# A block-sparse attention with two feed-forward layers: all steps in another searched order

## The chip, the cores and the metric

The kernel runs on one core of a Trainium2 chip. The metric is the time of the whole program on the device in microseconds (us), the median of three runs. The names of the engines are those of the profile: PE is TensorE (matmuls), PEld its weight loads, DVE is VectorE, ACT is ScalarE, POOL is GpSimd, and SP is SyncE, whose queue issues every DMA of this kernel.

## The reference, cut to what matters

```
# q, k, v: 2 batches x 8 heads x 768 positions x 64
k_sum = max of k over blocks of 32; v_sum = mean of v over the same blocks
scores = concat(local scores, banded to |i-j| < 16;  q @ k_sum + log(32)) / sqrt(64)
a = softmax(scores);  attn = a @ concat(v, v_sum)
x = attn as 1536 tokens x 512
h = x @ w_in (512 x 2048);   g = relu(h)**2;            x = g @ w_out (2048 x 512)
h = x @ w_in2;   g = h if h >= 1 else 0 if h <= -1 else (h+1)**2/4;   out = g @ w_out2
```

## The kernel before, in words

The attention is cut into 24 units, one for each pair of heads and each 256 queries. A unit has a score product (`S`, line 602), a max with mask (`M`, 610), an exponential (`E`, 616), a division (`R`, `N`), a transposition (`T`, 632), a value product (`O`, 643) and a split of the result into a high and a low part (`oh`, `ol`). These products are plain float32. Before the first value product the sums of `v` over the blocks must stand in the value tile (`v`, `vj`, and `f` on line 675).

The feed-forward products run as three products of high and low parts. Layer 1 begins with 24 units of 256 tokens (`H` on line 280 upwards, `Y` on line 407 downwards), which are mixed with the attention units. All other upward products (`Pa` to `Pg`, line 312) are one-level Strassen products of six matmuls, 384 tokens wide. Their sums and copies in PSUM are done by ACT and DVE (`Ca`, `Cc`, `Vb`, `Vc`, then `ha`, `hb`, `hc`, `hh`, `hl` for the activation and the split). A `Y` unit of layer 1 has 12 matmuls of 384 columns (256 in the mixed part). A `Y` unit of layer 2 has 9 matmuls of 512 columns.

The weights arrive as float64. For each of 64 tiles there is a load (`wl`, line 201), two steps on ACT (`dl`, `dq`), three on DVE (`dr`, `ds`, `dt`: lines 214, 216, 218), one on POOL (`da`, line 221) and a split (`wh`, line 235, and `wo`, line 240), with more sums for the Strassen products (`sa`, `sh`, `sl`).

The results of layer 2 are added up in SBUF (`ya`, line 432) and stored by rows of 128 tokens (`yd`, line 446). The last 128-token rows of the last group are made by four `Z` units (line 464: `Z0` and `Z1` are 12 matmuls of 512 columns, `Z2` and `Z3` the two halves of the third row block with 12 of 256), added by `za` (line 468) and stored by `zd` (line 473).

What sets the order is a table written out by hand, `PLAN`. It has one word for each step, and the program issues the steps in that order, each on its own engine. An engine works off its instructions strictly in that order, and so does SP's queue: a store that waits for its addition holds every DMA behind it. The last letter of a word (a, v or g) chooses ACT, DVE or POOL where a step can run on more than one.

Of the kernel before, what the change touches and what calls it, by code (L numbers as in the profile page):

```python
# [61 lines left out]
warm11 kl0 cl0 qf0 kl1 wl0 kl3 cl1 qf1 kl2 ql1 nl0 wl1 vl0 vl1 vl2 wl2 kl5 wl3 km0 S0 M0 km1 S1 E0 M1 dl0 km3 S3 dq0  # L62
E1 dr0 R0 M3 N0g km2 S2 E3 R1 ds0 N1g S5 M2 dq1 T1 R3 E2 N3v dt0 T3 T0 M5 da0 S7 to3a to0v E5 R2 S4 M7 N2g v0 dr1 T2
E7 wh0v v1 M4 wo0g R5 E4 R7 ds1 to1v v2 dt1 S6 N5v vc0 R4 dq2 wh1v vj0 N4g M6 vk0 dl1 vf0 vf1 ql2 wl4 dr2 E6 wl5 f0v
da1 kl6 to2v O0 ds2 O2 oh0v dt2 T4 oh2a O3 R6 to4a ol0 N6g oh3v dq3 O4 ol2 dl2 T5 ol3 dr3 S8 oh4a wl6 da2 ql3 vf2 f1a
ol4 to5a M8 O1 wh2a wo1g O5 oh1a T6 oh5a ol1 H1 dq4 ds3 wo2g to6v E8 ol5 S10 dr4 dt3 O6 N7v dl3 ds4 T7 dl4 M10 wl7 da3
bl0 kl4 vl3 wh3a S9 to7a dt4 H0 oh6a dq5 R8 ol6 E10 N8g M9 O7 S11 wo3g ha0v T8 ha1v oh7v hb1 wh4v da4 hb0 km5 dl5 hh0a
ol7 H2 hh1a dr5 hl0g to8a M11 E9 H3 hl1g ds5 wo4g km4 O8 S12 R10 ha2a ha3a R9 Y0 hb2 dt5 N9g oh8a hh2a km6 dq6 H4 E11
M12 hl2g da5 T9 vs0 S13 Y1 ha4a wh5a to9a bl1 dq7 wl8 Y2 wo5v wl9 ql4 kl7 vp0 vl4 hb3 dr6 E12 dr7 R11 H5 N10v N11g M13
# [732 lines left out]
```

## Time and profile before

| | us |
|---|---|
| median of 3 runs (lowest, highest) | 595.39 (595.04, 596.54) |
| the profiled execution | 594.42 |
| its span, first to last instruction | 592.6 |
| PE busy in the span | 569.6 |
| DVE, ACT, POOL busy | 474.7, 373.9, 243.5 |
| last matmul ends | 582.2 |

The profiled execution took 1.8 us more than its span and 0.97 us less than the median. "Busy" counts an engine's own instructions. Waits and DMA issues are not in it.

### The profile page before, as it was taken

What the parts mean: (1) busy time and instruction counts of PE and PEld (TensorE: products, weight loads), DVE (VectorE), ACT (ScalarE), POOL (GpSimd) and SP (SyncE); (2) the same over time, 40 slices, a digit from 0 to 9 for tenths busy, and PEclk for the clock granted to TensorE, in tenths of its full rate; (3) what the DMA queues carried; (4) which work ended last, traced back from release to release, by engine and by line L of the source; (5) the groups of instructions that cost most, each with busy time, mean ns of one, the idle gap of its engine ahead of it and who ended that gap; (6) DMA issues with size and microseconds to landing.
All of it is one profiled execution on the core that took longest, in us unless ns stands there. A gap on an engine that the chain in (4) does not pass through costs nothing.

```text
span 592.6 us, 11185 instructions
## 1 busy us (share of the span) xinstructions
PE 569.6 (96%) x4202; PEld 527.9 (89%) x4202; DVE 474.7 (80%) x1097; ACT 373.9 (63%) x866; POOL 243.5 (41%) x207
## 2 busy tenths in 40 slices
PE   6889999999999999999999999999999999999992
PEld 3578999999999999999999999888898998989982
DVE  5989889889989899768788999779897979666541
ACT  5778778757766455334657688877776656664430
POOL 0456464746563443415555566433431425121000
PEclk7899999999999999999999999999999999999997
DMA  8795711222122222112110302222211112000005
GB/s 321 283 297 133 228 46 40 90 72 73 71 72 72 107 107 72 71 51 94 72 72 1 117 26 72 71 72 71 89 54 72 72 36 105 3 1 2 1 1 212
DMA packets 16418, 52.17 MB, mean 88 GB/s; under 512 B 2124, under 2 KB 2732, under 8 KB 16364
## 3 DMA queue, kind: packets, MB, share of 16 engines
q1 hardware_dynamic: 16364, 51.45, 25.1%
q8 instruction: 33, 0.54, 0.4%
q14 instruction: 21, 0.17, 0.1%
HBM read 47.37 MB, written 3.15 MB: 85 GB/s over the span
## 4 chain that ended last, share of the span: by engine, by line
PE 84%; DVE 6%; DMA 5%; ACT 2%; issue 1%; SPq 0%; ACTq 0%; DVEq 0%
PE bank L407 40%; PE bank L312 31%; PE bank L280 5%; PE bank L602 3%; DMA raw<-in_wd_dram 2%; PE bank L632 2%; PE bank L643 2%; DMA k<-in_kd_dram 2%; PE bank L464 1%; DMA q<-in_qd_dram 1%; DVE fx L214 1%; DVE ks L590 1%; DVE fx L218 1%; DVE s L610 1%; ACT fr L207 1%
## 5 line engine op out<-in xcount | busy, mean ns | idle before, releaser
L221 POOL TENSOR_TENSOR fr<-fx,fr 128x512 uint32<-128x512 uint32 x64 | 84.6, 1333 | 152.6 <-DVE fx L218 82.9
L375 DVE TENSOR_TENSOR gl<-bank,gh 128x384 fp32r<-128x384 f32 (+1 forms) x124 | 65.8, 538 | 14.2 <-ACT gh L371 12.9
L312 PE MATMUL bank<-xh,wih 128*128 128x384 f32 x224 | 75.8, 339 | 0.5 <-DVE bank L325 0.5
L312 PE MATMUL bank<-xl,wih 128*128 128x384 f32 x224 | 75.2, 336 | 0.0
L350 ACT ACTIVATE tm<-bank,bias 128x384 f32<-128x384 f32 x62 | 35.9, 579 | 50.7 <-PE bank L312 41.2
L407 PE MATMUL bank<-gh,woh 128*128 128x384 f32 (+1 forms) x288 | 66.2, 321 | 0.0
L407 PE MATMUL bank<-gl,woh 128*128 128x384 f32 (+1 forms) x288 | 65.1, 317 | 0.0
L407 PE MATMUL bank<-gh,wol 128*128 128x384 f32 (+1 forms) x288 | 65.1, 317 | 0.0
L212 ACT ACTIVATE fx<-raw 128x512 f32<-128x512 f32 x64 | 42.5, 670 | 25.3 <-DMA raw<-in_wd_dram 19.5
L312 PE MATMUL bank<-xh,wil 128*128 128x384 f32 x224 | 57.1, 335 | 0.0
L312 PE MATMUL bank<-th,wih 128*128 128x384 f32 x168 | 56.3, 335 | 0.2 <-DVE bank L319 0.2
L312 PE MATMUL bank<-tl,wih 128*128 128x384 f32 x168 | 56.4, 336 | 0.0
L407 PE MATMUL bank<-woh,gh 128*128 128x512 f32 x180 | 56.0, 392 | 0.0
L407 PE MATMUL bank<-wol,gh 128*128 128x512 f32 x180 | 56.0, 392 | 0.0
L407 PE MATMUL bank<-woh,gl 128*128 128x512 f32 x180 | 56.0, 392 | 0.0
L432 DVE TENSOR_TENSOR acc<-bank,acc 128x384 f32<-128x384 f32 (+1 forms) x81 | 47.1, 603 | 8.7 <-PE bank L407 8.6
L367 DVE SCALAR_TENSOR_TENSOR bank<-bank,tm 128x384 f32<-128x384 f32 x64 | 35.5, 561 | 23.1 <-ACT tm L363 23.0
L407 PEld LDWEIGHTS bank<-gh,woh 128*128 128x128 f32 x288 | 48.9, 188 | 0.6
L407 PEld LDWEIGHTS bank<-gh,wol 128*128 128x128 f32 x288 | 49.0, 189 | 0.0
L407 PEld LDWEIGHTS bank<-gl,woh 128*128 128x128 f32 x288 | 49.0, 189 | 0.0
L207 ACT ACTIVATE fr<-raw 128x512 uint32<-128x512 uint32 x64 | 42.3, 668 | 5.8 <-DVE fx L216 2.1
L218 DVE SCALAR_TENSOR_TENSOR fx<-raw,fx 128x512 uint32<-128x512 uint32 x64 | 44.7, 706 | 0.4
(147 smaller groups left out, 1431.2 us busy)
## 6 DMA issues: line engine op xcount, KB each, us to landing
raw<-in_wd_dram SPq DMA_DIRECT2D x64, 512.0 KB, 4.6
k<-in_kd_dram SPq DMA_DIRECT2D x8, 400.0 KB, 6.5
out_dram<-acc SPq DMA_DIRECT2D x11, 256.0 KB, 2.8
q<-in_qd_dram SPq DMA_DIRECT2D x5, 512.0 KB
vw<-in_vw_dram SPq DMA_DIRECT2D x3, 768.0 KB, 7.0
vw<-in_vw_dram SPq DMA_DIRECT2D x2, 1024.0 KB
acc<-in_vb_dram SPq DMA_DIRECT2D x2, 768.0 KB
acc<-in_vw_dram SPq DMA_DIRECT2D x1, 1024.0 KB
```

The source lines that it names most:

```text
L207: A.activation(fr[n % 2], w_raw(n, 0), AF.Copy, scale=2.0 ** -29)
L212: A.activation(f32(x), f32(hi), AF.Abs)
L218: V.scalar_tensor_tensor(x, hi, 0xC0000000, x, ALU.bitwise_and, ALU.bitwise_or)
L221: G.tensor_tensor(fr[n % 2], fx[n % 2], fr[n % 2], ALU.add)
L280: PE.matmul(h_bank(n), a, b, start=i == 0, stop=i == len(ops) - 1)
L312: PE.matmul(q_bank(q, role), a, b, start=bool(first and i == 0), stop=i == 5, skip_group_check=not first)
L350: A.activation(a, h, AF.Relu, bias=bias[:, 1:2], scale=-1.0)
L367: V.scalar_tensor_tensor(h, h, 1.0, a, ALU.max, ALU.mult)
L375: e.tensor_tensor(lo, h if m else a, f32(hi), ALU.subtract)
L407: PE.matmul(ys[j], a, b, start=f == 0 and i == 0 and (n >= 24 or j % 2 == 0), stop=f == GF - 1 and i == 2 and (n >= 24 or j % 2 == 1))
L432: V.tensor_tensor(a, y_bank(g, t, j), a, ALU.add)
L602: PE.matmul(sbank(i, 2 * h + t)[r * 64:r * 64 + 64, 0 if keys else KW:KW if keys else KN], qs[cc % 2][rows, p, j * QT:(j + 1) * QT], b, st ...
```

## The change

Only the table `PLAN` changes. It holds the same 2277 steps, each once, with the same counts on the chip. They stand in another order, and of the steps that can run on several engines some run on another one. In the tail of the table the stores moved behind the additions that they need:

```
-hc133 ha135a hh133v Y129 hb135 hc135 hh135a Y130 hl135 hc134 hh134a Y131 ya104 hl134 ya106 hl133 Z0 Z3 Z1 za3 ya105 Z2
-za1 za0 zd1 yd105 yd101 yd96 zd3 yd104 yd100 yd98 yd102 yd106 yd97 za2 zd2 zd0
+ha135a hc134 hl131 Y129 hh134v hb135 hc135 hh133v Y130 hh135v hl135 hl134 ya102 Y131 ya104 hl133 yd104 yd101 yd100
+ya105 Z0 ya106 yd106 yd96 yd98 Z1 za0 zd0 yd102 yd97 yd105 Z2 za1 zd1 Z3 za2 zd2 za3 zd3
...
```

The end of SP's queue, before. L201 is the last load of weights, L473 a store of the last row blocks (`zd`), L446 a store of another row block (`yd`):

```order
L201 DMA raw_75<-in_wd_dram 128x1024 [waits DMAHW3_49]
L473 DMA out_dram<-acc 128x512 [waits DVE_49,Pool_49]
L446 DMA out_dram<-acc 128x512 x3
L473 DMA out_dram<-acc 128x256
L446 DMA out_dram<-acc 128x512
L446 DMA out_dram<-acc 128x512 [waits DMAHW5_49]
L446 DMA out_dram<-acc 128x512 [waits DMAHW6_49]
L446 DMA out_dram<-acc 128x512 [waits DMAHW7_49]
L446 DMA out_dram<-acc 128x512 [waits DMAHW0_49]
L446 DMA out_dram<-acc 128x512 [waits DMAHW1_49]
L473 DMA out_dram<-acc 128x256 [waits DMAHW2_49,DVE_49]
L473 DMA out_dram<-acc 128x512 [waits DMAHW3_49]
```

The same place now, without that load:

```order
L446 DMA out_dram<-acc 128x512 [waits DVE_49,Pool_49]
L446 DMA out_dram<-acc 128x512 [waits Pool_49]
L446 DMA out_dram<-acc 128x512
L446 DMA out_dram<-acc 128x512 [waits DVE_49]
L446 DMA out_dram<-acc 128x512 x2
L473 DMA out_dram<-acc 128x512 [waits DMAHW5_49,DVE_49]
L446 DMA out_dram<-acc 128x512 [waits DMAHW6_49]
L446 DMA out_dram<-acc 128x512 [waits DMAHW7_49]
L446 DMA out_dram<-acc 128x512 [waits DMAHW0_49]
L473 DMA out_dram<-acc 128x512 [waits DMAHW1_49,DVE_49]
L473 DMA out_dram<-acc 128x256 [waits DMAHW2_49,DVE_49]
L473 DMA out_dram<-acc 128x256 [waits DMAHW3_49,DVE_49]
```

Before, the first of the 13 stores is `zd1`, and it waits for `za1` on DVE. Now the first is `yd104`, which waits for `ya104`, and the four `zd` stand in the order in which their `Z` units end.

The first step on weights among DVE's work, before, as its 24th instruction. L590 is a maximum of a tile of `k`, L610 the mask and maximum of a score unit, L621 and L622 the division, L214 a step on the first tile of weights:

```order
L610 ISA sm_138 128x1
L590 TENSOR_REDUCE ks_123<-k_115 128x24
L214 TENSOR_SCALAR fx_76<-fx_76 128x512
L621 TENSOR_SCALAR sm_137<-sm_137 128x4
L622 RECIPROCAL sm_137<-sm_137 128x4
L610 ISA s_131,sm_140<-bank_65,cst 128x120
```

Now it is the fifth (L216, L218 and L235 are the next steps on the same tile):

```order
L214 TENSOR_SCALAR fx_76<-fx_76 128x512
L590 TENSOR_REDUCE ks_120<-k_112 128x24
L216 TENSOR_SCALAR fx_76<-fx_76 128x512
L218 SCALAR_TENSOR_TENSOR fx_76<-raw_74,fx_76 128x512
L590 TENSOR_REDUCE ks_123<-k_115 128x24
L235 CAST wih_80<-fx_76 128x512
L590 TENSOR_REDUCE ks_121<-k_113 128x24
L610 ISA s_128,sm_137<-bank_68,cst 128x120
```

The work on the first tile of weights, whose load is now the first DMA, moved ahead of the first score units' maxima.

A piece of the difference on PE in layer 2, between two `Y` units (L407), where two Strassen products (L312) are taken out and put elsewhere:

```order
 L407 MATMUL bank_63<-wol_86,gh_90 128x512
-L312 MATMUL bank_67<-th_1919,wih_81 128x384
-L312 MATMUL bank_67<-tl_1920,wih_81 128x384
-L312 MATMUL bank_67<-th_1919,wih_81 128x384
-L312 MATMUL bank_67<-tl_1920,wih_81 128x384
-L312 MATMUL bank_67<-th_1919,wil_83 128x384 x2
-L312 MATMUL bank_68<-xh,wih_1605 128x384
-L312 MATMUL bank_68<-xl,wih_1605 128x384
-L312 MATMUL bank_68<-xh,wih_1605 128x384
-L312 MATMUL bank_68<-xl,wih_1605 128x384
-L312 MATMUL bank_68<-xh,wil_1606 128x384 x2
 L407 MATMUL bank_65<-woh_84,gh_88 128x512
```

The two `Y` units around it now follow each other. Counted over the table, a `P` run is followed by a `Y` run 34 times in layer 2, and 44 times before. Between float32 attention products and the high-low products PE changes 35 times, and 47 times before.

## Rows read from the trace of the kernel before

**Rows 1.** The page: busy time, share of the span, instructions, by engine

```profile
PE 569.6 (96%) x4202; PEld 527.9 (89%) x4202; DVE 474.7 (80%) x1097; ACT 373.9 (63%) x866; POOL 243.5 (41%) x207
```

**Rows 2.** Windows: length, busy of PE, PEld, DVE, ACT, POOL, granted clock, DMA share, GB/s

```profile
0.00:15.00 15.00, 9.30 (x135) 5.46 (x139) 7.79 (x38) 7.73 (x28) 1.43 (x6) 0.78 0.88 323
15.00:30.00 15.00, 12.13 (x218) 7.80 (x210) 13.96 (x66) 10.75 (x46) 6.75 (x6) 0.84 0.76 280
30.00:45.00 15.00, 13.09 (x260) 11.23 (x260) 13.19 (x47) 11.69 (x34) 8.56 (x7) 0.93 0.92 296
45.00:60.00 15.00, 13.68 (x185) 12.82 (x179) 13.95 (x48) 12.43 (x45) 8.78 (x9) 1.00 0.54 133
60.00:575.00 515.00, 514.28 (x3388) 484.40 (x3387) 423.10 (x895) 331.31 (x716) 217.95 (x181) 1.00 0.19 65
```

**Rows 3.** PE's waits over the span: waited for, us, times, longest

```profile
PE bank L643 <- DVE vw L675: 2.9, 1, 2.9
```

**Rows 4.** DVE from 15 to 60 us, by form: busy us, mean ns, idle before

```profile
L218 DVE SCALAR_TENSOR_TENSOR fx<-raw,fx 128x512 uint32<-128x512 uint32 x7 | 4.7, 678 | 0.0
L216 DVE TENSOR_SCALAR fx<-fx 128x512 uint32<-128x512 uint32 x6 | 4.7, 784 | 0.0
...
L681 DVE TENSOR_REDUCE acc<-acc 96x64 f32<-96x2048 f32 x1 | 2.3, 2275 | 0.0
...
L635 DVE COPY pt<-bank 120x512 f32<-120x512 f32 x3 | 2.1, 688 | 0.4 <-PE bank L632 0.4
```

**Rows 5.** DVE from 60 to 580 us, by form

```profile
L240 DVE TENSOR_TENSOR wol<-fr,woh 128x512 fp32r<-128x512 f32 x13 | 9.7, 752 | 0.6 <-PE bank L407 0.6
```

**Rows 6.** Waits of SP's queue over the span

```profile
SPq L473 <- DVE acc L468: 80.9, 1, 80.9
...
SPq L797 <- DMA out_dram<-acc: 2.1, 1, 2.1
```

**Rows 7.** SP's timeline at the end: start, length, what (each is a DMA's issue)

```profile
581.53 0.35 SPq L473 DMA_DIRECT2D out_dram<-acc  x1
...
587.86 1.28 SPq L473 DMA_DIRECT2D out_dram<-acc  x2
```

**Rows 8.** DVE's timeline at the end

```profile
572.50 0.69 DVE L432 TENSOR_TENSOR acc<-bank,acc 128x512 f32<-128x512 f32 x1 [1.52 <-PE bank L407]
...
578.02 0.42 DVE L468 TENSOR_TENSOR acc<-bank,acc 128x256 f32<-128x256 f32 x1 [3.00 <-PE bank L464]
...
580.76 1.85 DVE L468 TENSOR_TENSOR acc<-bank,acc 128x512 f32<-128x512 f32 x3 [1.73 <-PE bank L464]
```

**Rows 9.** PE's timeline at the end, first matmul of Z0 and of Z3

```profile
573.66 0.39 PE L464 MATMUL bank<-woh,gh 128*128 128x512 f32 x1
...
576.38 0.28 PE L464 MATMUL bank<-woh,gh 128*128 128x256 f32 x1
```

**Rows 10.** The stores: us from issue to landing

```profile
DMA to landing us min/median/max: 2.4/2.8/3.1
```

**Rows 11.** The chain that ended last: start, us, what; from 60 us

```profile
79.75 1.62 PE bank L280 x12
...
119.20 1.44 PE bank L280 x12
...
312.12 2.38 PE bank L312 x12
...
347.94 2.08 PE bank L407 x9
350.02 1.06 PE bank L312 x6
...
460.10 4.18 PE bank L312 x24
...
563.58 10.24 PE bank L407 x45
573.83 8.34 PE bank L464 x48
```

More of the change, by code (lines that the diff above doesn't have):

```diff
@@ L157 @@
[L157 to L160 removed]
+warm11 wl0 kl0 qf0 kl3 kl1 cl0 qf1 wl1 ql1 kl2 wl2 vl0 nl0 vl1 vl2 wl3 dl0 dq0 dr0 km0 ds0 dt0 km3 da0 S0 wh0v wo0g
@@ new lines @@
+km1 S1 M0 dl1 M1 S3 E1 M3 E0 R1 km2 S2 N1g E3 R0 S5 M2 ql2 kl4 cl1 N0g T1 M5 dq1 S7 dq2 dr1 R3 E2 ds1 N3v T0 dt1 T3
+dr2 v0 E5 da1 to3v M7 v1 R2 ds2 dl2 S4 wh1v to1a wo1v E7 to0v R5 dt2 v2 N2v wh2a da2 M4 T2 vc0 dq3 R7 vj0 S6 to2v vk0
+N7g E4 M6 vf0 vf1 kl5 wl4 ql3 wl6 kl6 wl5 kl7 vf2 N5g f1v f0v O1 E6 R4 O3 N4v O2 dr3 T4 ds3 O0 to4a oh2v R6 oh0a ol2
+T5 N6g oh1a ol0 S8 oh3a ol1 to5a ol3 O4 dq4 M8 wo2g T6 oh4a S9 to6a ol4 dr4 E8 S10 dt3 T7 M9 O5 H1 ds4 oh5a to7a ol5
+R8 dl3 dt4 O6 dl4 da3 M10 H0 E9 bl0 wl7 oh6v N8g ol6 km5 S11 ha0a da4 O7 wh3a ha1v T8 hb1 oh7v hh1a R9 ol7 H2 wh4a
@@ new lines @@
+to13a R15 ug0v dl8 dq9 dr8 Y7 ub0v yo7a N14v S16 ds8 ol12 yo5a S17 O13 M16 ha9a T14 hb9 H10 oh13a hh9v hb8 M17 hl9g
+hh8a hl8v N15g E17 Y8 to14v ol13 uh0v H11 E16 R17 dt8 S18 uc0v S19 ha11a R16 ui0a dr9 O14 N16g M18 T15 oh14a Y9 ha10a
+to15v uj0g E18 ol14 M19 O15 ds9 T16 N17g hb11 oh15v S20 hb10 ol15 to16a R18 S21 E19 da8 T17 M21 O16 N18g H12 M20 E21
+uk0v H15 dt9 oh16a to17v wl11 hh10a wl10 da9 vl5 S23 E20 ol16 R19 S22 ul0v O17 N19g T18 LW0 wh8a M22 H14 hh11a to18a
+wh9v um0a R20 wo9g oh17v H13 hl11v ha12a saa2g ol17 dq10 R21 hl10g E22 O18 ha14v wo8v sab2g T19 Y10 un0v N20g hb12
@@ new lines @@
+hl18 ug1g wo10v Y17 hb19 wh13a da13 ha21v dl12 hh19v Y18 hl19 ds12 dt12 H22 ue0v wh12a wl14 da12 hb21 hh21a Y19 ha20v
+wo13v uh1g wo12v H23 saa3g ui1a Pc0 hb20 uj1v ha22a sab3v hb22 Pb0 yo19a Cc0v uk1v Pd0 dq15 Vb0 ul1g ha23a dr15 hh20a
+Pf0 hh22a sac3v sh7a hl20 Y20 dq14 hl21 sl7g hl22 ha24a dr14 um1a hb23 Y21 un1g ha25v ds14 hb25 sad3g hh23a Pa1 hb24
+hl23 hh25a uo1g hh24v Pe0 hl24 hl25 up1g Y22 Vc0 uq1v ha26a dt14 hb26 Y23 ds15 Ca1a sh6v hh26a dt15 sl6g hl26 Pd1
+yo23v ur1g Pc1 dl14 wh15v wh14a wl16 Pb1 ua2g Cc1a ha28v dl15 Pg0 hb28 ub2g Vb1 wl17 Pf1 da14 ha27v hh28v Pe1 uc2v
@@ new lines @@
+Pb5 dr25 dq24 wo23v Cc5a dr24 Y39 dl25 ds25 Vb5 hh43a ds24 ya14 Pd5 ya13 ya12 Pf5 dt25 ha44v da25 Pe5 hl43 ha45a ya15
+hb44 hb45 dt24 Y40 hh44a wl26 wh25a wl27 da24 hl44 hh45a wh24v wo25g Pa6 wo24v Y41 saa6v hl45 sab6g Vc5 Ca6a sac6v
+ha46a Pg5 sad6g hb46 dq27 hh46v Pb6 ha47a hl46 sh12v sh13v Pc6 sl13v Pd6 Cc6a hb47 Vb6 Y42 hh47v ha48a dr27 hb48 sl12v
+hh48a hl47 dl27 ds27 Y43 dt27 ya16 wh27a wl29 da27 dq26 Pf6 ya19 wo27g ya18 Pa7 hl48 ha49v dr26 Pe6 hb49 ya17 dl26
+ds26 Y44 dt26 Vc6 wl28 da26 hh49v ha50a wh26a Pg6 dq29 wo26v hb50 dr29 Y45 hl49 Ca7v dq28 ha51a dr28 Pd7 hh50a ds29
@@ new lines @@
+hb51 ds28 dt29 hh51a Y46 dl29 wh29v dt28 wl31 da29 ha52v hl50 hb52 Pb7 hh52a wo29g dl28 hl52 Pc7 hl51 wl30 da28 Y47
+Cc7a dq31 ya20 Vb7 wh28v saa7v Pe7 wo28g ya23 dq30 Pf7 Vc7 sab7g ya21 Pg7 dr31 sac7g Pa8 sad7v ha55a dr30 ha53a ya22
+hb55 Y48 sh15a hb53 sl15v sh14a ha54v sl14v Y49 hb54 hh53a hh55v dl30 ds31 hh54a hl54 Y50 hl55 hl53 Ca8a Pb8 Y51 ya25
+ds30 Pc8 dt30 ya26 wl32 Pd8 ya24 ya27 Cc8v Y52 ha56a dt31 dl31 Vb8 hb56 wl33 da31 wh30a hh56v Y53 hl56 da30 wh31a Pf8
+dq32 dr32 wo30v Pe8 ha57a dq33 Y54 hb57 dr33 wo31v hh57a Vc8 hl57 ha58a Pg8 ds32 hb58 dt32 dl33 Pa9 hh58v ds33 hl58
@@ new lines @@
+Y55 dt33 ha59v wh33a da33 Ca9a ya29 dl32 Pc9 hb59 wo33v wl34 da32 wl35 ya28 Pb9 wh32v Cc9a Pd9 Vb9 wo32v Pf9 ha60a
+ya30 saa8v hb60 ya31 Pe9 hh60a sab8g ha61v hl60 sac8g Y56 dq35 hh59v dq34 sad8g Vc9 sh17a hl59 hb61 dr35 sl17g sh16a
+Y57 ds35 dl35 dr34 dt35 hh61a Pg9 ha62a da35 Pa10 ha63v hl61 hb63 Y58 hb62 Ca10v wh35a hh62v hh63a hl62 ds34 sl16v
+Pc10 dt34 Pd10 Cc10a dl34 Pb10 wh34a ha64v wl36 da34 wl37 hl63 hb64 Y59 Vb10 wo35g ya32 yb32a hh64a wo34g ya34 Pf10
+ya33 ya35 yc32g Y60 hl64 yb34v ha65v dq37 dq36 Pe10 yb35a dr36 dl37 dr37 yb33v dl36 Y61 ds37 yc33g Vc10 hb65 ds36
@@ new lines @@
+ds39 Y68 dt39 hh72a hb73 hl72 wl41 da39 yb41a Vc12 wh38v Y69 hc73 dq40 ha74a dr40 wo38v Y70 wh39v hb74 yc41v yb42a
+hc74 yb40a ds40 hh74a wo39v dl40 Y71 yc40v dq41 dt40 dl41 dr41 wl42 da40 hh73a ya45 yb43a Pa13 ya44 wh40a ds41 uf4g
+ya46 Pg12 ya47 yb46a hl74 Y72 ha75a dt41 hl73 ui4a wl43 da41 Ca13v wh41a Pc13 ua4v dq42 wo41g hb75 Pb13 Cc13a hc75
+yb47a yc42g hh75a Pd13 Vb13 dq43 wo40v yc43g Pf13 ha76a hl75 Pe13 uj4g hb76 ha77a hc76 Pa14 hh76v saa10g hb77 Y73 hl76
+hc77 yc46g Vc13 hh77a yc47v ha78a sab10v Pg13 uk4v hb78 Y74 sac10v um4a hl77 dr43 Ca14a un4g hc78 ha79a hh78v Pd14
@@ new lines @@
+Pf17 sab12v ya60 sac12g Pg17 ha93a dr50 sad12g ds50 Y88 hb93 sh25v ha94a dt50 hc93 Y89 sl25v hh93a hb94 hl93 ha95a
+dr51 hc94 sh24v Y90 dl51 hh94v hb95 ds51 Ca18a hl94 dt51 Pd18 hc95 wh51a wl53 da51 hh95v Pc18 ha96a hl95 sl24g Pb18
+Cc18v hb96 wh50a hc96 Y91 wo51v dq53 ya64 dl50 Vb18 hh96a wl52 da50 dl53 Pa19 hl96 wo50g Pe18 Pf18 Vc18 ya65 ha98a
+Pg18 dr53 ds53 dq52 Y92 ha97a dr52 dt53 wl55 hb97 dl52 Y93 hc97 hh97a ha99a hl97 ds52 Y94 dt52 Ca19a hb98 ya66 wl54
+da52 hb99 hc98 wh52v hh98a Pd19 wh53a hl98 wo52g hc99 Pb19 ha100a da53 Pc19 hh99a hb100 Y95 hc100 Cc19a wo53v hh100a
@@ new lines @@
+Vb19 saa13g hl99 hl100 sab13g Pf19 ya68 sac13g sh27v Pe19 ha101a sad13v sl27g ya70 Pa20 ya69 Y96 Vc19 ha102a hb101 Y97
+hb102 hc101 hc102 hh101a hh102a hl101 hl102 Ca20a Pg19 sh26v sl26g Pc20 ha103a Pd20 Cc20a hb103 Pb20 dq55 hc103 dl54
+dr55 Y98 dq54 hh103a dr54 ha104a Vb20 ds54 hl103 Y99 dl55 ds55 ya72 dt55 Pf20 ya73 da55 dt54 Pa21 ha105a ya74 Pe20
+wl56 wl57 da54 hb104 hb105 hc104 Y100 hc105 hh104a hh105v hl104 wh54a Vc20 Y101 hl105 dq56 ha106a wh55v wo54v dq57
+Y102 wo55v hb106 Ca21a dr57 dl57 ds57 hc106 Pd21 dt57 hh106a dr56 wl59 Pg20 da57 hl106 ha108a wh57v Pb21 hb108 ds56
@@ new lines @@
+wo57g ha107a hc108 Pc21 dt56 saa14g hh108v Y103 Cc21a hl108 dq59 Vb21 dl56 wh56v hb107 ya76 wl58 da56 Pf21 ya77 hc107
+Pe21 wo56g hh107a ha109a Y104 Vc21 sab14v hl107 hb109 dq58 hc109 ha110a dr59 Pa22 ds59 dr58 Pg21 dt59 hb110 hc110 Y105
+hh109v ha111a hl109 Ca22v hh110a sac14v hb111 sh29v Y106 sad14v sl29g hc111 sh28a ds58 hh111a wh59a Pd22 hl110 dt58
+Pc22 sl28v ha112a Pb22 Cc22v dl59 hl111 hb112 wl61 da59 Y107 dl58 hc112 Vb22 hh112a wl60 da58 ya80 wh58a hl112 Pe22
+Pf22 dq61 Vc22 ya81 ha114a Pg22 ya78 ha113a Pa23 hb114 Y108 hb113 hc114 hc113 hh114a dq60 hl114 hh113a Y109 ha115a
@@ new lines @@
+hl113 dr60 dr61 Ca23a ya82 hb115 Pb23 ds61 wo59v ds60 Pd23 dl61 dt60 dt61 Pc23 ha116a hc115 wl63 da61 Y110 hb116 hc116
+wo58g hh116v Cc23v Y111 dl60 Vb23 hh115a hl116 wl62 da60 wh61v Pf23 hl115 wo61v Pe23 saa15v ha117a sab15g Pa24 Vc23
+wh60a ya85 dq63 Pg23 ya84 dq62 wo60v ha118a Y112 sh31a hb117 sl31g hb118 hc117 Y113 ha119a sac15g sad15g hh117a Y114
+hl117 hc118 Ca24a hb119 hh118v hc119 Pd24 hl118 ya86 Pc24 ha120a Pb24 hh119a Cc24a hl119 Y115 hb120 Vb24 sh30a dr62
+ya88 hc120 Pf24 sl30v hh120v Pe24 hl120 ha121a ya89 Pa25 Vc24 hb121 hc121 Pg24 hh121a ha122a Y116 ha123v hb122 Y117
@@ new lines @@
+hc122 hb123 hh122v dr63 hl121 Y118 Ca25v hl122 ya90 hc123 Pb25 ds62 hh123v Pc25 ds63 dt62 hl123 Pd25 Cc25v Vb25 Y119
+ha124a ya92 hb124 hc124 Pf25 ya93 hh124a hl124 Pe25 ha125a dt63 Pa26 Vc25 wh62a ya94 hb125 Pg25 ha126a hc125 hh125v
+Y120 dl63 hl125 hb126 da63 Ca26v hc126 hh126a Pd26 ha127a hl126 Pb26 hb127 dl62 Pc26 hc127 ha128a da62 Y121 Cc26v
+wh63a Vb26 wo62g hb128 hh127a hl127 Pf26 wo63g hc128 Pe26 ha129a Pa27 hb129 hh128a hc129 Y122 hl128 hh129a hl129 Y123
+ya96 ya97 Y124 Ca27v ya98 Vc26 ha130a Y125 hb130 hc130 Pd27 hh130a hl130 Pg26 ha132a Pb27 ha131v Pc27 Y126 Cc27v hb131
@@ L161 @@
+hb132 hc132 Vb27 Y127 hh132v hl132 ya100 hc131 Pe27 ya101 hh131a Pf27 Vc27 ha134v Pg27 ha133a Y128 hb133 hc133 hb134
+ha135a hc134 hl131 Y129 hh134v hb135 hc135 hh133v Y130 hh135v hl135 hl134 ya102 Y131 ya104 hl133 yd104 yd101 yd100
+ya105 Z0 ya106 yd106 yd96 yd98 Z1 za0 zd0 yd102 yd97 yd105 Z2 za1 zd1 Z3 za2 zd2 za3 zd3
 """
```

132 lines of the change are left out of this document (35 added, 97 removed).

## The prediction

> **What bounds the kernel now.** I read the busy line first: PE is busy for 569.6 of 592.6 us [rows 1]. The windows then say where the other 23 us lie [rows 2]. From 60 to 575 us PE is idle for 515.00 − 514.28 = 0.72 us, so there only the matmuls themselves cost time. In the first 60 us it is idle for 5.70 + 2.87 + 1.91 + 1.32 = 11.8 us. From 15 us on DVE is busy for 41.1 of 45 us there, the longest wait of PE is one of 2.9 us for DVE, at the first value product [rows 3], and the granted clock is 0.78, 0.84 and 0.93 of full speed, which costs 15 × (0.22 + 0.16 + 0.07) = 6.8 us of clock at most. The loads take 0.88, 0.76 and 0.92 of the DMA engines. At the end 10.4 us pass after the last matmul (582.2 to 592.6). SP's waits and its timeline show what fills them: one store waits 80.9 us for an addition on line 468 [rows 6], is issued at 581.53, and the last of the 13 issues ends at 587.86 + 1.28 = 589.14 [rows 7]. The last landing is awaited for 2.1 us more [rows 6], and 592.6 − 589.14 − 2.1 = 1.36 us close the span.
>
> So the kernel has three places where an order can win or lose: the head, where DVE is late; the middle, where PE is full; and the tail, where SP works off stores while nothing else runs.
>
> **The tail.** The first of the stores is now `yd104`. Its addition ended at 572.50 + 0.69 = 573.2 before [rows 8], and one `Y` unit fewer stands behind the last `P` run, so it ends at about the same time. From then on SP can issue. Even at 0.64 us for one (the slower of the rows, 1.28 for two [rows 7]), the ten stores of `yd` need 6.4 us and are out by 579.6. PE's matmuls are the same and the last one still ends at 582.2. A `Z` of 512 columns takes 576.38 − 573.66 = 2.72 us [rows 9]. In the new order `Z0` ends at 576.4, `Z1` at 579.1, `Z2` at 580.7 and `Z3` at 582.2. The additions, 0.69 us for 512 columns and 0.42 for 256 [rows 8], follow at 577.1, 579.8, 581.1 and 582.6, and each `zd` stands behind its own. Only `zd3` is left after the last matmul: an issue of 0.35 [rows 7] ends at 583.0, and 2.1 us of waiting [rows 6] give 585.1. From the rows on landing the same store lands 2.8 us after the issue begins, 3.1 at most [rows 10]: 585.45 or 585.75. With the closing 1.36 the span ends between 586.4 and 587.1. I take 586.6, which is 6.0 us less. The bounds are −5.0 (the last four issues at 0.64 us and the slowest landing) and −6.5 (the fastest landing, 2.4 us).
>
> The trace lands its stores, issued one behind another, in 2.4 to 3.1 us [rows 10]; the new last store is nearly alone. The Trainium skill ("DMA: Bandwidth & Descriptors", section "Latency and other measured facts") says that a lighter load on HBM makes the fixed cost of a DMA smaller. By it the lone store would land at the low end or below it, and the sum would be some 0.4 us less than by the median. No run here shows a lone store yet, and I keep the median.
>
> **Fewer changes of kind on PE.** All durations are of the chain. A `Y` run of layer 2 takes 2.08 us for one unit (9 matmuls) and 10.24 for five (45), so a unit is 2.04 and the start of a run 0.04. A `P` run takes 1.06 for one and 4.18 for four (24), so a unit is 1.04 and a start 0.02 [rows 11]. A pair of runs less saves 0.06 us; ten pairs fewer (44 to 34) save 0.6. In the mixed part a block of 12 matmuls of line 280 among float32 products takes 1.62, against 1.44 among its like [rows 11]: 0.18 for two changes. Twelve changes fewer, six such blocks, save 1.1. I take −1.6 for both. The bounds are −1.7 and 0: in the head the saving is worth nothing where PE waits for DVE anyway.
>
> **The head.** SP now begins with 128x1024 of weights ahead of the first `k` and `q`, and DVE begins with four steps on that tile. Two things follow. The first score product starts later, by the time of one load in a queue that moves 323 GB/s [rows 2]: 512 KB take 1.6 us, less the 192 KB of constants that went behind `q`, 0.6 us, which leaves 1.0. And DVE has, ahead of the first value product, one more each of lines 216, 218, 240 and 635: 0.78 + 0.68 + 0.75 + 0.69 = 2.9 us [rows 4, 5]. The first two belong to the first tile and can run in the 7.2 us in which DVE is idle before 15 us [rows 2]. What is left is 1.4 us, so I expect that wait at 4.3 us in place of 2.9 at the outside. Up to the first `Y` unit DVE's work grows by one reduction of line 681, 2.28, and two of line 240, 1.50, less one each of 216 and 218, 1.46 [rows 4, 5], and shrinks by some shorter steps whose rows I do not add up: 2.3 at the most, and I judge 0.9. PE's own work up to there falls by one `H` block, 1.44 [rows 11], and a score product, but this work is only done later and saves nothing by itself. In the other direction the start of weights in DVE's idle 7.2 us can take work out of the stretch from 15 to 60 us, where DVE is full: four steps, some 2.9 us. That bounds the head by −2.9 below, and above by 2.3 + 1.0 = +3.3. I take +0.9, nearest to the difference in the work that DVE has before it.
>
> **The middle.** PE idles 0.72 us from 60 to 575 us, so a gain is bounded by that and by the refilling of the array that goes with such a stop; one is in the row of 12 matmuls of line 312 that took 2.38 us [rows 11], where two units need 2 × 1.04 + 0.02 = 2.10. Longer runs of `P` ask ACT and DVE for sums and copies of one unit after another, and the weights of layer 2 are asked for earlier. DVE has 515 − 423 = 92 us free there [rows 2], which covers steps that only change places. If a run outpaces it, the price is a wait like the one of 2.9 us [rows 3], the longest wait of a product for DVE. I take 0, between −0.7 and +2.9.
>
> **Sum.** Against the profiled execution of 594.42 us: −6.0 − 1.6 + 0.9 + 0 = −6.7, which is 587.7. The profiled execution lies 0.97 us under the median of 595.39, so the forecast is 588.7.
>
> **Rivals.**
> - *The tail is not shortened.* A store near the front of the new list waits for an addition on POOL (`yd104` and `yd101` wait for DVE and POOL), or a `zd` is held by a queue that still has a store in flight, and the issues bunch behind the last matmul as before. For it: before, an issue takes up to 0.64 us and each needs its queue free. Against it: the rows give 6.4 us for ten stores and there are 9 us from 573.2 to 582.2. Time: 588.7 + 6.0 = 594.7, no change.
> - *Slower: the head.* DVE reaches the first value product so late that PE stands still there and then works on at the lower of its two levels, 1.2 in place of 2.4 GHz, for one more stretch. For it: the granted clock is 0.78 to 0.93 in just these windows [rows 2], behind PE's waits, and the first `q` comes later. Against it: the additional work is 1 to 3 us, beside waits of 11.8 us in all. Price: a stretch of 10 us of work at half clock costs 5.0 us, the wait of 1.4 + 1.0 comes first, and the matmuls that then stand behind DVE another 3: 9.4 us in place of 0.9, so 597.2. It decides only from a loss of 1.8 + 6.7 + 0.9 = 9.4 us in the head. The Trainium skill ("TensorE: Matmul & The Clock Gate", section "HAM oscillation — how this bites in real kernels") describes waits between bursts of matmuls that put the array back to half its clock each time; the windows of the head agree, with 0.78 and 0.84 where PE waits most.
> - *New stops in the middle.* A longer run of `P`, or a weight tile that is asked for earlier, makes PE wait. For it: DVE is busy for 82% of the middle. Against it: 0.72 us of idle in 515. One or two waits of up to 2.9 us: 591 to 593.
> - *The head gains.* DVE uses its idle first 15 us: −2.9 in place of +0.9 gives 584.9; half of that 586.8.
>
> **How the numbers follow.** Chances: the forecast (587 to 590.5) 0.58, the gaining head 0.16, stops in the middle 0.14, the tail not shortened 0.07, the slower head 0.05. About 0.3%, 1.8 us, can be told from no change here, so faster is below 593.6 and slower above 597.2. The first three cases are faster, 0.88; the tail's rival is the same, and some of the head's, 0.08 together; 0.04 is slower. The range takes in the gaining head down to 585.0 and the stops in the middle up to 592.3.
>
> **What would show it.** Right: SP's issues start near 573 and the last ends near 583; no wait of 80.9 us; the span ends 4 to 5 us after the last matmul; more rows of 18 or more matmuls on lines 312 and 407; PE busy is less by about 1. The wait at line 643 tells the head: over 5 us, or a mean clock under 0.78, 0.84 and 0.93 in its windows, speaks for the slower head, a shorter wait for the gain. PE idle from 60 to 575 us over 2 us would show new stops. The forecast is wrong if the last matmul ends after 584 or before 578, or if more than one store is issued after it.

## The result, and the profile after

| | before | after |
|---|---|---|
| median, first comparison (us) | 595.96 (595.04 to 597.64, 4 runs) | 589.0 (587.68 to 589.47, 4 runs) |
| ratio, 95% interval | | 0.9876 [0.9848, 0.9905] |
| median, timed again later | 596.46 (593.64 to 598.08, 11 runs) | 587.09 (585.89 to 590.81, 6 runs) |
| ratio, 95% interval | | 0.9852 [0.9826, 0.9877] |
| profiled execution, its span | 594.42, 592.6 | 589.21, 586.9 |
| from the last matmul to the end of the span | 592.6 − 582.2 = 10.4 | 586.9 − 583.41 = 3.5 |

The change makes the kernel faster by 1.2 to 1.5%, 7 to 9 us; 588.7 us was forecast. All of the gain in the two spans (5.7 us) lies behind the last matmul, which itself ends 1.2 us later than before. The forecast had it 0.7 us earlier (−1.6 + 0.9 + 0). In a second profile of the changed kernel (e12 below) the last matmul ends at 581.2 us, 1.0 earlier than before, and the span is 584.7 us: 3.5 us lie behind it again. Outside the span the changed kernel takes longer than the kernel before, 589.21 − 586.9 = 2.3 us against 594.42 − 592.6 = 1.8. Every run of the two has about this difference, the forecast does not have it, and what makes it stays open.

The page's busy line of the changed kernel, which answers to [rows 1]:

```profile
PE 572.8 (98%) x4202; PEld 528.6 (90%) x4202; DVE 473.4 (81%) x1089; ACT 375.5 (64%) x877; POOL 235.4 (40%) x203
```

The windows of the changed kernel, in the columns of [rows 2]:

```profile
0.00:15.00 15.00, 9.16 (x115) 5.06 (x115) 7.81 (x38) 5.68 (x18) 2.73 (x6) 0.79 0.86 319
15.00:30.00 15.00, 14.20 (x160) 8.24 (x160) 11.91 (x55) 10.34 (x43) 5.68 (x5) 0.50 0.76 296
30.00:45.00 15.00, 12.50 (x254) 9.40 (x254) 10.92 (x47) 10.12 (x37) 3.38 (x4) 0.91 0.67 228
45.00:60.00 15.00, 14.96 (x234) 13.84 (x232) 14.24 (x46) 12.49 (x44) 10.30 (x10) 1.00 0.63 171
60.00:575.00 515.00, 513.60 (x3402) 484.85 (x3399) 425.17 (x901) 336.89 (x740) 213.34 (x179) 1.00 0.20 66
```

PE is idle for 9.2 us in the first 60 (11.8 before), but from 15 to 30 us it works at a granted clock of 0.50 (0.84 before): it is busy for 14.2 us and does 160 matmuls where 218 were done before. That is why PE is busy for 3.2 us more in all, and not for 1 less. In the second profile it is busy for 569.4 us, 0.2 less than before.

The tail of the changed kernel: first SP's issues (start, us, what), then SP's waits behind 560 us, then the end of the chain of waits:

```profile
574.53 4.26 SPq L446 DMA_DIRECT2D out_dram<-acc  x6
578.89 0.40 SPq L473 DMA_DIRECT2D out_dram<-acc  x1
579.34 1.77 SPq L446 DMA_DIRECT2D out_dram<-acc  x3
581.28 2.93 SPq L473 DMA_DIRECT2D out_dram<-acc  x3
```

```profile
SPq L446 <- DVE acc L432: 74.2, 2, 73.9
SPq L473 <- DVE acc L468: 1.6, 2, 1.0
SPq L797 <- DMA out_dram<-acc: 1.5, 1, 1.5
```

```profile
575.09 8.32 PE bank L464 x48
583.41 0.02 issue
583.43 0.42 DVE acc L468
```

A wait of 73.9 us still stands in SP's list, but it is now the first store's, and it ends at 574.5 where the wait of 80.9 us [rows 6] ended at 581.5. The stores go out beside the `Z` products. After the last addition (583.85) one issue is left, which ends at 581.28 + 2.93 = 584.21; its landing is awaited for 1.5 us, against 2.1 [rows 6].

To see where PE loses and gains between 0 and 575 us, I counted for several traces how much of PE's work was not yet done at a moment, every step at the duration that is usual for it. The table gives how far a kernel is behind the profiled execution of the kernel before (us, worked out from all of PE's rows; negative is ahead). "Changed, again" is the second profile, e12. The row at 100 us stands among steps of many kinds and is good to some 0.5 to 1 us, the others to about 0.2.

| at (us) | changed | changed, again | e1 | e2 | e4 | e9 | e10 | e11 |
|---|---|---|---|---|---|---|---|---|
| 60 | 2.1 | 0.8 | −0.1 | 0.4 | 2.4 | −2.0 | 0.1 | −0.6 |
| 100 | 2.5 | 1.1 | 0.2 | 0.4 | 3.5 | −1.7 | 0.3 | −0.3 |
| 240 | 2.1 | 0.1 | 2.1 | 1.8 | 5.6 | −2.7 | 3.1 | −0.6 |
| 400 | 1.7 | −0.3 | 0.9 | 1.8 | 4.7 | −3.2 | 2.5 | −0.8 |
| 573 | 1.3 | −0.9 | 1.0 | 1.2 | 4.7 | −3.2 | 2.5 | −1.2 |

### The profile page after: what moved, and what is told of

Its sections match the earlier page's. It is cut to its first block, busy times and chain, and to the rows that moved or that the text cites. A ratio compares the mean times of both kernels' runs of the same rounds, so it can differ in the third digit from the quotient of the medians.

```text
span 586.9 us, 11206 instructions
## 1 busy us (share of the span) xinstructions
PE 572.8 (98%) x4202; PEld 528.6 (90%) x4202; DVE 473.4 (81%) x1089; ACT 375.5 (64%) x877; POOL 235.4 (40%) x203
## 4 chain that ended last, share of the span: by engine, by line
PE 89%; DVE 7%; DMA 2%; ACT 1%; POOL 1%; issue 0%; SPq 0%; ACTq 0%; DVEq 0%; POOLq 0%
PE bank L407 42%; PE bank L312 33%; PE bank L280 5%; PE bank L602 3%; PE bank L632 2%; PE bank L643 2%; PE bank L464 1%; DMA k<-in_kd_dram 1%; PE bank L665 1%; DMA raw<-in_wd_dram 1%; DVE ks L590 1%; DVE acc L681 1%; DVE s L610 1%; DVE fx L214 1%; DVE fx L216 0%
## 5 line engine op out<-in xcount | busy, mean ns | idle before, releaser
L221 POOL TENSOR_TENSOR fr<-fx,fr 128x512 uint32<-128x512 uint32 x64 | 86.1, 1350 | 208.2 <-DVE fx L218 95.8
L312 PE MATMUL bank<-xh,wih 128*128 128x384 f32 x224 | 75.4, 337 | 0.2 <-ACT bank L319 0.2
L312 PE MATMUL bank<-xl,wih 128*128 128x384 f32 x224 | 75.3, 336 | 0.0
L407 PE MATMUL bank<-gh,woh 128*128 128x384 f32 (+1 forms) x288 | 66.2, 320 | 0.2 <-DVE acc L432 0.2
L407 PE MATMUL bank<-gh,wol 128*128 128x384 f32 (+1 forms) x288 | 65.2, 317 | 0.0
L407 PE MATMUL bank<-gl,woh 128*128 128x384 f32 (+1 forms) x288 | 65.1, 317 | 0.0
L312 PE MATMUL bank<-xh,wil 128*128 128x384 f32 x224 | 57.1, 336 | 0.0
L312 PE MATMUL bank<-th,wih 128*128 128x384 f32 x168 | 56.4, 336 | 0.0
L312 PE MATMUL bank<-tl,wih 128*128 128x384 f32 x168 | 56.4, 335 | 0.0
L407 PE MATMUL bank<-woh,gl 128*128 128x512 f32 x180 | 55.9, 392 | 0.0
L407 PE MATMUL bank<-woh,gh 128*128 128x512 f32 x180 | 55.9, 392 | 0.0
L407 PE MATMUL bank<-wol,gh 128*128 128x512 f32 x180 | 55.8, 391 | 0.0
L407 PEld LDWEIGHTS bank<-gh,woh 128*128 128x128 f32 x288 | 49.0, 189 | 0.8 <-DVE acc L432 0.6
L407 PEld LDWEIGHTS bank<-gh,wol 128*128 128x128 f32 x288 | 49.0, 189 | 0.2 <-DVE wol L240 0.2
L407 PEld LDWEIGHTS bank<-gl,woh 128*128 128x128 f32 x288 | 49.0, 189 | 0.0
L218 DVE SCALAR_TENSOR_TENSOR fx<-raw,fx 128x512 uint32<-128x512 uint32 x64 | 47.2, 742 | 0.5
```

The source lines that it names most:

```text
L218: V.scalar_tensor_tensor(x, hi, 0xC0000000, x, ALU.bitwise_and, ALU.bitwise_or)
L221: G.tensor_tensor(fr[n % 2], fx[n % 2], fr[n % 2], ALU.add)
L312: PE.matmul(q_bank(q, role), a, b, start=bool(first and i == 0), stop=i == 5, skip_group_check=not first)
L407: PE.matmul(ys[j], a, b, start=f == 0 and i == 0 and (n >= 24 or j % 2 == 0), stop=f == GF - 1 and i == 2 and (n >= 24 or j % 2 == 1))
```

## The experiments

In the first four a table begins in one of the two orders and goes on with the steps still missing in the other. The line numbers of e1 to e4 are higher by 3.

**e1_tail_new**: 2253 steps of before, then the new end.

```
-ya106 hl133 Z0 Z3 Z1 za3 ya105 Z2 za1 za0 zd1 yd105 yd101 yd96 zd3 yd104 yd100 yd98 yd102 yd106 yd97 za2 zd2 zd0
+hl133 yd104 yd101 yd100 ya105 Z0 ya106 yd106 yd96 yd98 Z1 za0 zd0 yd102 yd97 yd105 Z2 za1 zd1 Z3 za2 zd2 za3 zd3
```

> The kernel before with only the last 24 steps of the table in the new order (the stores behind their additions); the first 2253 steps as before. Theory, from the two traces: the stretch from the last matmul to the end shrinks from 10.4 to 3.5 us, so -6.9 us, about 589.0 for 595.9, ratio 0.988, which is the whole gain of the change. Rival 1, the term of the prediction: -6.0. Rival 2: the tail is not what made it faster (half or less, -3.5 or less; ratio above 0.994) and the rest of the order did.

Measured: 589.14 us against 595.55, −6.4 us by the medians; ratio 0.9886 [0.9871, 0.9902], which is −6.8 us (−5.8 to −7.7). The stretch from the last matmul to the end:

```profile
583.11 0.02 issue
583.13 0.42 DVE acc L471
```

The span is 586.7, so it is 3.6 us. With the old tail it is 10.4 us in the profile of before, and 10.9 and 10.5 in those of e4 and e10. So the tail alone gives most of the gain: rival 2 is out by the time. Between the theory's −6.9 and rival 1's −6.0 the time does not decide; the stretch does, with −6.8.

**e2_layer2_new**: 1482 steps of before (to the start of layer 2), then the new order.

```
-... hl79 ds42   (old order to the end)
+... hl79 ds43   (new order to the end)
```

> The kernel before up to the start of layer 2 (1482 steps), then the new order: longer runs of one kind in layer 2, and the new tail. Theory: ten pairs of runs fewer save 0.6 to 0.8 us on PE beside the tail's 6.9: -7.6, ratio 0.987. Rival: longer runs save nothing that lasts, the same as the tail alone (-6.9).

Measured: 589.07 us, ratio 0.9894 [0.988, 0.9907]; by time it can't be told from e1. From 400 to 573 us it gains 1.8 − 1.2 = 0.6 on PE, e1 none (0.9 and 1.0), but it entered that stretch 0.9 behind e1. The saving is there on PE and not to be seen in the time. A part of it is lost outside the span, which takes 2.3 us in e2 (588.97 − 586.7) and 1.9 in e1 (588.57 − 586.7).

**e3_head_old**: 309 steps of before (to about 75 us), then the new order.

> The kernel before for the first 309 steps (to about 75 us: loads, first attention units, first Y units), then the new order. Theory: the new head costs 2 to 3.5 us (PE's work is that far behind in the trace from 60 us on), so with the old head the rest gains -9 to -10: 586 to 587, ratio 0.984. Rival: the lag of the head is a matter of one execution (its clock was 0.979, others of the same kernel had up to 0.997), and this kernel takes as long as the changed one, -7.0, ratio 0.988.

Measured: 590.18 us, ratio 0.9912 [0.989, 0.9934], slower than both readings. Its chain at 74 us shows why:

```profile
74.25 0.34 SPq L579
...
75.72 4.75 DMA vw<-acc
80.48 0.14 issue
80.61 0.69 PE bank L646 x16
```

SP waited with the load of queries (L579) for a score product, and the fills of the value tile queued behind it came 2.5 us late for PE. The place is the seam's (where the two orders are joined), so e3 does not price the head. e5 tries to mend it.

**e4_head_new**: 309 steps of the new order, then the order before with its old tail.

> The new order for the first 309 steps, then the order before, with its old tail. Theory: slower than before by 2 to 3.5 us, 598 to 599.5, ratio 1.0035 to 1.006. Rival: the head's order is free, ratio 1.000. Second rival: the head itself gains (the mixed part with fewer changes of kind), ratio 0.998.

Measured: 598.11 us, ratio 1.0037 [1.0022, 1.0052]: +2.6 by its median. In this mixed table, with the old rest, the new head loses, as the theory had it. Its profile is of the slowest of its seven runs.

**e5_head_old_ql5**: e3 with one load moved.

```
-... ql5 vf4 vf3 ol11 H8 ...
+... vf4 vf3 ql5 ol11 H8 ...
```

> The kernel of the experiment with the old head (old order for 309 steps, then the new one), with one load moved: the last load of queries (ql5) behind the two fills of the value tile (vf4, vf3). In that experiment SP waited for a score product with this load at 74 us, and PE stood still for 2.5 us at 78 to 81 us for the fills queued behind it. Theory: that wait is a fault of the seam, it goes, and the time falls by 2.5 us from 590.2 to 587.7, ratio 0.987; then the old head is worth 1.3 us over the new one with the same rest. Rival: another wait takes its place (DVE is full to 66 us there) and the time stays above 589, ratio 0.9895 or more.

Measured: 587.92 us, ratio 0.9866 [0.9842, 0.9891]. The time came where the theory had it, but not by its mechanism. In PE's timeline the wait is only shorter, 1.85 us for 2.5:

```profile
77.88 0.69 PE L643 MATMUL bank<-pt,vw 120*64 120x64 f32 x16 [1.85 <-DMA vw<-acc]
```

Copies of the value sums (L687), which themselves stood behind a load of `k`, hold the fills now: another wait took the place of the first, as the rival said, though not at the rival's time. And the profiles of e3 and e5 part before the moved load: at 60 us they are 2.1 and 0.2 us behind, with the same steps up to there. So the 2.3 us between the two medians can't be put down to the load, and what the old head is worth under the new rest is not shown by e3 or e5.

**e6_loads_before_fill** and **e7_more_warm**: the changed kernel with two loads moved, and with more dummy matmuls (`warm`: matmuls ahead of PE's first product or in its gaps, whose results nothing reads).

```
-M6 vf0 vf1 kl5 wl4 ql3
+M6 kl5 wl4 vf0 vf1 ql3
```

```
-warm11 ... S0 ... S1 ... S3 ... S2 ...
+warm14 ... S0 warm3 ... S1 warm2 ... S3 warm2 ... S2 warm1 ...
```

> The changed kernel with two loads (kl5 and the weights wl4) moved ahead of the first fill of the value tile (vf0), on whose wait of 15.2 us SP's queue stood while the DMA engines were empty from 27 to 32.6 us. Theory A: the empty DMA engines are what the new head loses; 912 KB are loaded there, and the kernel gains 1 to 2 us: 587 to 588, ratio 0.985 to 0.987. Theory B: DVE's own work is the bound of the head (the chain lies on DVE from 49 to 66 us without a gap), the earlier loads gain nothing: 589.0, ratio 0.9885.

> The changed kernel with 11 more dummy matmuls in PE's gaps of the first 16 us (three at the start, three, two, two and one behind the first score products), which leave the results alone. In the trace of the changed kernel PE works at 1.2 GHz from 8.6 to 32.4 us. Theory A (the slower rival of the prediction): the clock is what the head loses; with the clock held the lag of 2 to 3.5 us is gone, 586 to 587, ratio 0.984. Theory B: the clock is hidden behind loads and DVE, as another execution with the same head at full clock came to 60 us no earlier; 589.0, ratio 0.9885, with a granted clock of 0.95 or more in the windows from 0 to 30 us.

Measured: 586.81 us, ratio 0.9846 [0.982, 0.9872], and 587.06 us, ratio 0.9851 [0.9823, 0.9878]. Both look like theory A. They are not, as e12 shows. In e7's profile the clock was not held either (0.90 and 0.65 in the first two windows), and among its runs the fastest, 585.56 and 585.92, have the mean clock 0.997, the slowest, 588.9, has 0.984. One sentence of e7's expectation rests on a reading that fell later: the "full clock" of e4's head (see the last section).

**e8_new_from_390us**: 1625 steps of before, then the new order.

> The kernel before up to 391 us (1625 steps), then the new order: the longer runs of layer 2 without the stretch from 342 to 391 us, where PE stops for 0.3 to 0.6 us in the new order. Theory: PE full from 391 to 573 us in both, so the fewer pairs of runs show: last matmul 0.4 to 0.6 us earlier against the lag at 391 us than with the old order, total with the new tail -7.0 to -7.5 us, ratio 0.988. Rival: runs cost nothing, lag unchanged from 391 to 573 us, the same as the tail alone.

Measured: 589.57 us, ratio 0.989 [0.9862, 0.9918]. Counted as in the table, from 400 to 573 us it goes from 0.2 behind to 0.5 ahead. That is about the forecast 0.6 on PE, and again not to be seen in the time beside e1 (589.14). Outside the span e8 takes 2.2 us (587.54 − 585.3).

**e9_loads_and_warm**, **e10_before_warm** and **e11_no_warm**: the edit of e6 with still more dummy matmuls; the kernel before with more; the changed kernel with one.

```
e9  warm17 ... S0 warm8 ... S1 warm3 ... S3 warm3 ... S2 warm1 ...
e10 warm13 ... S0 warm6 ... S1 warm3 ... S3 warm6 ...
e11 warm1
```

> The changed kernel with both earlier edits of its head: the two loads (kl5, wl4) ahead of the first fill, and more dummy matmuls (17 at the start, then 8, 3, 3 and 1 behind the first score products; 21 more than in the changed kernel). With 11 more, the time of single runs followed the clock: 585.6 to 586.5 at 0.994 to 0.997, 587.6 to 588.9 at 0.984 to 0.988. Theory A: clock and loads are two separate losses of the head, and they add up: 584 to 585, ratio 0.981. Theory B: both shorten the same chain, and the time stays where each alone had it: 586.0 to 587, ratio 0.9845.

> The kernel before with 17 more dummy matmuls in PE's gaps of the first 15 us (13 at the start, then 6, 3 and 6), nothing else. In its trace PE works at 1.2 GHz from 8.3 to 18.6 us and from 28.8 to 32.2 us. Theory A: the old head is bound by loads and DVE and loses nothing by the clock: 595.6, ratio 1.000. Theory B: the clock costs the old head too: -1 to -2 us, ratio 0.997.

> The changed kernel with one dummy matmul at the start instead of 11. Theory A: without the warm-up PE works at 1.2 GHz for most of the first 30 us in every run; as the changed kernel mostly does so already (from 8.6 to 32.4 us in its trace), it loses little: 589.0 to 589.8, ratio 0.9885 to 0.990. Theory B: the full clock in the first 8.6 us is worth a microsecond or more: 590.5 or more, ratio above 0.991.

Measured: e9 586.46 us, ratio 0.9845 [0.982, 0.9871]; e10 596.97 us, ratio 1.0018 [1.0003, 1.0033]; e11 587.31 us, ratio 0.9849 [0.9829, 0.9868]. In e9's profile PE is 2.0 us ahead at 60 us, the best head of all, and the span 582.2; but its six runs reach from 584.4 to 589.45 at clocks of 0.994 to 1.0. In the old head the held clock (1.00 and 0.99 in the first two windows) gains nothing (e10, theory A; its interval even lies just above 1). Taking the warm-up away does not hurt (e11): it came out lower than both of its readings, which were put on top of the changed kernel's first 0.9876.

**e12_after_again**: the changed kernel itself.

> The changed kernel itself, unedited, timed again beside the kernel before, since three edits of its head (two loads moved, more dummy matmuls, only one) all came to 0.985 and its own ratio, 0.9876, is of four runs. Theory A: these edits gain 1 to 2 us over it, and it comes to 0.987 to 0.989 again. Theory B: its first four runs lay high, and it comes to 0.985 as they do; then nothing done to the head is worth anything that these runs can tell.

Measured: 587.09 us, ratio 0.9852 [0.9826, 0.9877]. Theory B: no edit of the head is worth anything that these runs can tell, and no version was found that beats the changed kernel. What its two profiles show of the head is still instructive. First the first value product (L643) of the kernel before, then, of the changed kernel as profiled after the change and again, sums of the value blocks (L665) and the first value product:

```profile
28.34 1.85 PE L643 MATMUL bank<-pt,vw 120*64 120x64 f32 x32 [2.85 <-DVE vw L675]
```

```profile
22.33 3.64 PE L665 MATMUL bank<-vw,acc 96*32 96x512 f32 x16
...
34.73 0.69 PE L643 MATMUL bank<-pt,vw 120*64 120x64 f32 x16 [1.73 <-DVE vw L675]
```

```profile
23.09 2.23 PE L665 MATMUL bank<-vw,acc 96*32 96x512 f32 x16
...
32.61 0.69 PE L643 MATMUL bank<-pt,vw 120*64 120x64 f32 x16 [1.72 <-DVE vw L675]
```

Sixteen matmuls take 3.64 us where the array stays at 1.2 GHz (granted clock 0.50 from 22 to 26 us) and 2.23 where it changes to 2.4 GHz on the way (0.56 from 22 to 24 us, 1.00 from 24 on), and the same program starts its first value product 2.1 us apart. At 60 us the one is 2.1 behind, the other 0.8.

## Why the prediction was right

*The tail* (−6.0 forecast, −6.9 measured). The order of events came as worked out, with one store after the last matmul. The term was small by 0.9. The forecast took 586.6 − 582.2 = 4.4 us from the last matmul to the end, the trace shows 3.5: addition 0.44, issue 0.36, landing 1.5 and closing 1.2. The landing is the most of it, 0.6: the 2.1 us were those of the last of 13 stores issued one behind another, and of 128x512. The new last store is of 128x256, half as many bytes. The Trainium skill ("DMA: Bandwidth & Descriptors", section "Latency and other measured facts") says that the fixed cost is smaller with less load on HBM. The trace agrees in the sign, 1.5 against 2.1 us, and the sum by its rule was the better one; but the size of the store changed with the load, and no run here parts the two. The forecast also counts ten stores of `yd` where there are nine, which changes nothing: SP began at 574.5 and had the last of them issued by 581.1, before the last matmul.

*The tail's rival* fell: the stores are not bunched behind the last matmul, and e1 has 6.4 to 6.8 us of gain by the tail alone.

*Fewer changes of kind* (−0.6 in layer 2, −1.1 in the mixed part). From 400 to 573 us kernels with the new order gain 0.4 to 0.6 us on PE (changed, again, e2, e11), those with the old order nothing (e1, e4, e10). That fits the price of a run's start. But e9, with the new order too, gains nothing there, with one wait of 0.3 us. The −1.1 of the mixed part is shown by no run. Of the twelve changes of kind that went, eight lie before 100 us, where their worth can't be told from the head's waits (by PE's rows 29 changes up to 100 us before and 21 now, 18 and 14 behind it), and the mixed part ends at 137 to 140 us. So what the table shows from 100 to 240 us is mostly not its work, and the row at 100 us is not exact enough for it. Of the −1.6, some −0.5 is shown.

*The head* (+0.9, bounds −2.9 and +3.3). PE is +0.8 and +2.1 behind at 60 us in two executions of the same program, and e4 is 2.6 us slower by its median (its profile is 2.4 behind at 60 us and loses as much again up to 573, mostly in the old middle). The sign was right and the size is near, but that was luck: the 0.9 was judged and not added up, and the working did not hold. I derived it from DVE's work, with a wait at L643 of 4.3 us as the mark. That wait is 1.7 us, shorter than before, although the first value product comes 4.3 and 6.4 us later. From the end of the products on line 671, whose result DVE hands on (L675), to the first value product it is 2.85 us before, and 2.8 and 2.4 in the two profiles of the changed kernel. Score products now stand in that time, so PE waits less. The mark could not tell what it was to tell.

The lateness begins before that place. The first score product waits for the first `q`, which comes later, as the prediction said (1.0 us). Before, then in the changed kernel:

```profile
6.16 0.40 PE L602 MATMUL bank<-k,q 64*64 64x96 f32 x8 [0.56 <-DMA q<-in_qd_dram]
```

```profile
7.33 0.40 PE L602 MATMUL bank<-k,q 64*64 64x96 f32 x8 [1.48 <-DMA q<-in_qd_dram]
```

That is 1.2 us; in the second profile it starts at 8.19, 2.0 us later. From there PE itself is slow in the first of the two profiles: busy for 14.2 of 15 us at a clock of 0.50, the level of 1.2 GHz. In the second the clock is 0.71 there, PE is busy for 12.25 us, and the longest wait on the way is one of 1.6 us for ACT (L235). The prediction's other mark, the clock, was under the rows of before in two of three windows (0.50 and 0.91 for 0.84 and 0.93) and spoke for the slower rival, where the wait spoke for the gain. That rival named the mechanism, at 9.4 us (its own terms, 5.0 + 1.4 + 1.0 + 3, make 10.4). It took place at a price of about 1.3 us, if the whole difference of the two profiles at 60 us is the clock's, and did not decide.

*The middle* (0, bounds −0.7 and +2.9). This is the step that failed, by its bound. I read from one profile that PE idles 0.72 us in 515, so no more could be gained. Other executions of the old order show more. The window from 140 to 245 us in the columns of [rows 2], first of the kernel before:

```profile
140.00:245.00 105.00, 104.78 (x619) 104.00 (x618) 92.18 (x185) 62.22 (x128) 51.44 (x46) 1.00 0.25 90
```

The same window of e1, which has the old order here too:

```profile
140.00:245.00 105.00, 103.35 (x609) 102.17 (x608) 91.52 (x183) 62.08 (x128) 50.66 (x45) 1.00 0.26 90
```

Of the changed kernel, and of its second profile:

```profile
140.00:245.00 105.00, 104.85 (x617) 104.04 (x616) 89.18 (x179) 60.27 (x131) 52.11 (x45) 1.00 0.21 71
```

```profile
140.00:245.00 105.00, 105.00 (x622) 104.72 (x621) 88.99 (x179) 60.01 (x130) 54.36 (x47) 1.00 0.21 73
```

With the old order in this stretch PE is idle for 0.22 us in the profile shown, and for 1.65 in e1 (e2 1.17, e4 1.75, e8 0.54, e10 2.14). With the new one it is idle for 0.15 and 0, and in the six other profiles that have it (e3, e5, e6, e7, e9, e11) for 0 to 0.24. The chain of e1 at that place:

```profile
227.92 0.59 ACT fr L210
...
228.52 4.76 DMA raw<-in_wd_dram
...
233.37 0.67 ACT fx L215
...
234.59 0.38 ACT tm L325
...
234.99 0.58 DVE bank L328
...
235.61 2.37 PE bank L315 x12
```

A load of weights is issued when ACT is done with its buffer (L210), takes 4.76 us, near the usual 4.6, and lands at 233.3. ACT, which works in order, is held by it, and the copy and the sum for the next Strassen product follow late. What set ACT back ahead of it is not shown. The table has much the same: four kernels with the old middle (e1, e2, e4, e10) lose 1.4 to 2.8 us between 100 and 240 us, four with the new one gain 0.3 to 1.0. Counted in the same way, e8 with the old middle loses only 0.4, and e6 with the new one loses 0.9. So the new order mends a stop of up to 2 us that varies from one execution to the next and that the one profile of before happened not to have. That it makes up for the head is a sum of these rows (+0.8 to +2.1 and −1 to −2). No experiment changed this place by itself.

The rival of new stops came true in small. In every profile that begins with the new order (changed, again, e4, e6, e7, e9, e11) a score product waits 1.1 us for DVE at 62 to 67 us, in the changed kernel here:

```profile
66.56 0.30 PE L602 MATMUL bank<-k,q 64*64 64x96 f32 x2 [1.08 <-DVE xl L656]
```

The kernel before has no such wait. So PE's idle time from 60 to 575 us rose from 0.72 to 1.40 us (1.09 in the second profile), under the 2 us that the prediction named as the sign.

*The whole*: −6.9 of the tail, −0.5 of the runs, about −1.5 of the middle's stop and +0.8 to +2.1 of the head make −6.8 to −8.1 against a usual execution, and −6.3 to −7.6 with the 0.5 us that the changed kernel loses outside the span; −7.0 and −9.4 were measured by the medians. Some 2 to 3 us of the second measure have no place in this account. The tail is shown by e1; the rest is argued from profiles. That the forecast of 588.7 lies between 587.1 and 589.0 is in part luck: the tail's and the middle's gains, both too small in it, stood against savings that were taken too large and a loss that was not in it.

## What to carry to other kernels

Look first at what one queue does behind the last product: here 13 stores stood behind one addition, 10.4 us for 3.5, and no other change of the order tried here came near that. One profile bounds a stop only for that execution: before you write that no more than 0.7 us can be gained, ask whether the slack of a late load (4.7 us of landing here) is as small as its variation. Price a new order's head by how much of the work is done at a fixed moment (0.8 to 2.1 us behind at 60 us here), not by how long the engine waits for one product (1.7 us for 2.9), nor by when that product starts (4.3 to 6.4 us later).

## What the runs showed of the hardware that was not expected

The granted clock can be recorded as 1.00 while PE works at the lower level. The first score product of e11, with one dummy matmul ahead, and the same product later:

```profile
7.41 0.60 PE L602 MATMUL bank<-k,q 64*64 64x96 f32 x8 [5.52 <-DMA q<-in_qd_dram]
...
25.00 0.40 PE L602 MATMUL bank<-k,q 64*64 64x96 f32 x8
```

The page says 1.00 for all of e11, but eight matmuls take 0.60 us at 7 us and 0.40 at 25, so it worked at 1.2 GHz first. In the kernel before the same eight take 0.58 us at 14.6 us, at a granted clock of 0.50, and 0.40 at 19.0, where it has risen to 1.00. e4's head was the same (0.60 us under a clock of 1.00), so the sentence in e7's expectation on "full clock" was wrong. The Trainium skill ("TensorE: Matmul & The Clock Gate", section "Seeing it yourself") warns that such events have been seen to be unreliable; these rows agree. Read the clock from the duration of equal matmuls.

Six runs of one program (e9) differ by 5.0 us, 584.4 to 589.45, at a mean clock between 0.994 and 1.0. The late load may be a part of it, but the one profile of e9, its fastest run, has no idle time from 140 to 245 us, so this is not shown; the cause stays open.
